# One fused attention and gated feed-forward kernel: a new planner order, pair sums, normalisation on three engines

## The chip, the cores and the metric
The kernel runs on one core of a Trainium2 chip. The metric is the device time of one execution in microseconds: 446.09 us, the median of three runs (445.58 to 446.64).

## What is computed
Attention over 4 batches, 8 heads, 768 positions and 64 columns, where a query sees the 96 positions up to its own and the first 8 keys, with a distance bias; its output feeds a feed-forward part (512 to 1024 to 512) with a gate.

```
scores = q @ k.T / 8 + bias            # bias = -2**-(h+1) * distance, -1e9 where not kept
a = exp(scores - max);  a = a / (sum(a) + 1e-9);  x = a @ v
h = relu(x @ w_in)                                   # 512 -> 1024
conv[s] = cw[0]*h[s-1] + cw[1]*h[s] + cw[2]*h[s+1]   # per column of h
out = (h * sigmoid(conv)) @ w_out                    # 1024 -> 512
```

w_in, conv_w and w_out arrive in double precision. Products are made in three parts of a high and a low half, so that they keep float32's precision.

## The kernel before, in words
The work is cut into 32 attention jobs (batch, half of the sequence, pair of heads) of three steps each, so 96 steps of 128 queries by two heads, and into 8 units of four jobs, each followed by its share of the feed-forward part. A step goes round the engines: TensorE makes both heads' scores (`s`, L512 to L515), VectorE adds the bias table and takes the maximum (L523), ScalarE takes the exponentials and their sums into columns of the small tile `mm` (L536), VectorE adds 1e-9 and inverts (`inverse`, L545 and L546), VectorE or GpSimd multiplies the weights by the inverse (`normalise`, L551), TensorE transposes them (`t`, L559 and L561), ScalarE evicts the transposes (`pt`, L566). Three steps make one product with v (`pv`, L576), whose high half ScalarE takes (`xh`, L586) and whose low half VectorE takes (`xl`, L591).

Of these, `mm1` (L602) makes the first feed-forward product in triples of matmuls per column block f of 8 and per job k of 4, into three accumulators; ScalarE's relu frees them (L610). Three taps follow per block: the middle one on GpSimd (L630), the outer two on VectorE (L632); then gate and saturation check on ScalarE, the gated product `c` (L664) and its low half `gl` (L682) on VectorE, and `mm2` (L692) makes the output tiles `o` of 24 matmuls. The very last tile is made in two halves `e` of 24 matmuls each (L720).

Sixteen pieces of the weights are taken apart during the first quarter (L445, L450, L455, L461). For a rare kind of input there is a general path behind a branch. Whether it is needed is found from the limits, the weights' words (16 checks, L477) and the saturation sums: VectorE reduces these (L481 to L490), one matmul sums the result over partitions (`total`, L771), VectorE writes the flag (L773), and all engines branch on it at the end.

The order on every engine is written by a planner (`Plan`, a list scheduler with hand-made costs and due times): each operation has an engine or a choice of engines, a cost, what it must follow, which buffers it takes, and when it is due; the cheapest start wins, and among those within 60 ns the earliest due. While the plan leaves TensorE a gap early on, filler matmuls on a zero tile (`warm`, L298) are put there. Loads go out on SyncE's queue, the first few also on ScalarE's.

Of the kernel before, what the change touches and what calls it, by code (L numbers as in the profile page):

```python
# [39 lines left out]
NPB, NPT = 4, 4  # L40
# [4 lines left out]
EARLY = 2  # L45
# [20 lines left out]
class Op:  # L66
    def __init__(self, key, eng, fn, after, alloc, use, due, behind):
        self.key, self.eng, self.fn, self.after, self.behind = key, eng, fn, after, behind
        self.alloc, self.use, self.due = alloc, use, due


RESULT = {"PE": 175, "ACT": 118, "DVE": 82, "POOL": 70, "SP": 900}
WAKE = {"PE": 45, "ACT": 45, "DVE": 45, "POOL": 90, "SP": 90}
ISSUE, SETUP, RATE = 570, 500, 270.0


class Plan:
# [8 lines left out]
    def best(self, free, taken):  # L86
        return self.arrange(free, taken)

    def arrange(self, free, taken):
# [21 lines left out]
        wire, port = free.pop("DMA"), {"DVE": 0.0, "POOL": 0.0}  # L111
        last_max, landed = False, [0.0] * LANES
        pe_gap = []
# [14 lines left out]
        while cand:  # L128
            best = None
            heads = {}  # L130
            for k in cand:
# [12 lines left out]
                for e, c in o.eng.items():  # L144
# [5 lines left out]
                    if c[1] and e in port:  # L150
                        t = max(t, port["POOL" if e == "DVE" else "DVE"])
# [5 lines left out]
            for e, hs in heads.items():  # L157
                t0 = min(h[0] for h in hs)
                _, due, k, c, t = min((h for h in hs if h[0] <= t0 + SLACK[e]), key=lambda h: (h[1], h[0]))
                if len(ops[k].eng) > 1:  # L160
                    mine = t + c[0]
                    others = [max(h[0], free[x]) + h[3][0] for x, g in heads.items() if x != e for h in g if h[2] == k]
# [11 lines left out]
            if k[0] in LOADS:  # L174
                free[e] = t + ISSUE
                wire = max(t + ISSUE + SETUP, wire) + c[0]
                end[k] = wire + RESULT["SP"]
                landed.append(end[k])
            else:
                free[e] = t + c[0]  # L180
                end[k] = t + c[0] + (150 if k[0] == "max" else RESULT[e])
                if c[1] and e in port:
                    port[e] = t + c[0]
# [22 lines left out]
EASY = 36000.0  # L206


def fast_path(tc, io):
# [43 lines left out]
    def load_q(m, j):  # L253
        b, u, hp = jobs[m]
        if m < NATIVE:
            r = slice(D * j, D * j + D)
            E = nc.sync if m else nc.scalar
# [31 lines left out]
    for m in range(2):  # L289
        zero_q(m)  # L290
# [3 lines left out]
    wp = ps_m.tile([P, 512], F32, tag="m", name="warm")  # L294

    def warm(n):
        for _ in range(n):
            T.matmul(wp[:, :P], wz, wz, start=True, stop=True)  # L298
# [20 lines left out]
    make_identity(nc, ident)  # L319
# [5 lines left out]
    V.tensor_scalar(lt, rel, 0.0, None, ALU.is_lt)  # L325
    nv = nn.rearrange("p (a b) -> p a b", a=2)
# [8 lines left out]
    W, M = slice(WIN, NT), slice(0, WIN)  # L335
    gW, gM = slice(WIN, WIN + NGLOB), slice(P - NGLOB, P)
# [7 lines left out]
    def nearer(r):  # L344
        V.tensor_scalar(rel[:, r], rel[:, r], nl, None, ALU.subtract)

# [4 lines left out]
    nearer(W)  # L351
    V.scalar_tensor_tensor(rel[:, gW], off[:, gW], 0.0, rel[:, gW], ALU.is_equal, ALU.mult)
    V.scalar_tensor_tensor(off[:, gW], keyf, ng, off[:, gW], ALU.is_ge, ALU.min)
    masked(W)
    for h in range(2):
        table(h, W)

    def middle():
        outside(M)
        nearer(M)  # L360
        V.memset(rel[:, gM], 0.0)
        V.tensor_scalar(off[:, gM], keyf, ng, None, ALU.is_ge)
        masked(M)
# [30 lines left out]

    cw = const.tile([P, 3 * NF], F32, name="cw")
# [18 lines left out]
    for t in pbuf:  # L414
        G.memset(t[:, 2 * WIN :], 0.0)

# [40 lines left out]
    def weight_low(i, half):  # L457
# [3 lines left out]
        V.tensor_tensor(l[:, sl], t, h[:, sl].bitcast(F32), ALU.subtract)  # L461
# [55 lines left out]
    def maximum(s, j):  # L517
        m, i, first, n = form(s)
        if j == 0:
            sums[s] = p1.tile([P, 8], F32, tag="mm", name=f"mm{s}", bufs=6)  # L520
# [12 lines left out]
    def exponentials(s, j):  # L533
# [4 lines left out]
            bias=mm[:, j : j + 1], scale=-1.0, accum_out=mm[:, 2 + j : 3 + j],  # L538
# [4 lines left out]
    def inverse(s):  # L543
        mm = sums[s]
        V.tensor_scalar(mm[:, 4:6], mm[:, 2:4], 1.0e-9, None, ALU.add)  # L545
        V.reciprocal(mm[:, 6:8], mm[:, 4:6])  # L546

    def normalise(s, j, eng):
        x = weights_of(s, j)
        X = V if eng == "DVE" else G  # L550
        X.tensor_scalar(x, x, sums[s][:, 6 + j : 7 + j], 1.0, ALU.mult, ALU.mult)  # L551

    def transposes(s, j):
        n = form(s)[3]
        pb = pbuf[s % NPB]
        if j == 0:
            st_pt[s] = ps_t.tile([P, 2, 2, P], F32, tag="t", name=f"t{s}")
        pt = st_pt[s]
        T.transpose(pt[:, 0, j], pb[:, j * WIN : j * WIN + P], ident)  # L559
        if n > P:  # L560
            T.transpose(pt[:, 1, j], pb[:, j * WIN + P : j * WIN + 256], ident)  # L561

    def evict(s):
        k = 1 if form(s)[2] else 2
        sb = p2.tile([P, 2, 2, P], F32, tag="pt", name=f"pt{s}", bufs=NPT)
# [3 lines left out]
    def values(m):  # L569
        pv[m] = ps_v.tile([P, TB], F32, tag="v", name=f"pv{m}")  # L570
        for i in (NB - 1, *range(NB - 1)):
            whole = form(NB * m + i)[2]
            sb = st_pt.pop(NB * m + i)
            for c, n, q in ((0, P, 0),) if whole else ((0, P, 0), (1, NLATE, NEAR)):
                for j in range(2):
# [3 lines left out]
                        sb[:n, c, j, q:],  # L579
# [16 lines left out]
    def mm1(n, f, k):  # L596
        if k == 0:
            hist["h", n, f] = ps_m.tile([P, 512], F32, tag="m", name=f"h{n}_{f}")
        ps = hist["h", n, f]
# [21 lines left out]
    def tap(n, f, k):  # L621
# [7 lines left out]
        if k == 1:  # L629
            G.tensor_scalar(c, h, x, 1.0, ALU.mult, ALU.mult)  # L630
# [44 lines left out]
    def low_g(n, t):  # L675
# [6 lines left out]
        V.tensor_tensor(  # L682
# [82 lines left out]
    def verdict():  # L765
        check_weights()
        check_gates()
        total = ps_v.tile([P, 512], F32, tag="v", name="total")
        E = mybir.EngineType
        hint = lambda e: tc.mark_branch_hint_location("general", "LikelyTaken", [e])  # L770
        T.matmul(total[0:1, 0:1], bad, ones, start=True, stop=True)  # L771
        hint(E.PE)
        V.tensor_scalar(flag[0:1], total[0:1, 0:1], 0.5, None, ALU.is_gt)  # L773
        hint(E.DVE)

    plan = Plan(dict(s=2, t=2, v=1, m=3, xh=6, xl=6, gh=4, gl=4, rk=1, rq=1, kk=2, ql=2, qh=2,
                     vv=2, pt=NPT, pb=NPB, mm=6, c=1, ob=1), ("ob",))
    add = plan.add
    act = lambda n, sb=0, bias=0, acc=0: ("ACT", (n * 0.833 + 50 + 45 * sb + 95 * bias + 93 * acc, 0))
    dve = lambda n: ("DVE", (n * 1.042 + 70, 1))  # L780
# [15 lines left out]
    for m in range(len(jobs)):  # L796
        native, w = m < NATIVE, NKC[jobs[m][1]]
        D0 = due_of(NB * m)
        if native:
# [4 lines left out]
            add(("ldk", m), ("SP", (P * w * 4 / RATE, 0)), (load_k, m), alloc=() if m % 2 else (bk,), use=(bk,), due=D0 - 9000)  # L804
            for j in range(2):
                add(("ldq", m, j), ("SP" if m else "ACT", (D * TB * 4 / RATE, 0)), (load_q, m, j),
# [336 lines left out]
```

## Time and profile before
| | |
|---|---|
| median of three runs | 446.09 us (445.58 to 446.64) |
| the profiled execution | 446.33 us |
| its span | 444.5 us |
| mean granted clock of TensorE | 0.992 of full |
| instructions | 8851 |
| HBM read, written | 52.95 MB, 6.29 MB |

The profile covers one execution. Busy time counts an engine's own instructions. Matmuls overlap, and their ends are modelled: what a matmul costs is the distance between two starts. "Idle before" names the engine whose result ended the wait.

### The profile page before, as it was taken

How to read it: one execution, taken by the hardware profiler on the slowest of the kernel's cores; microseconds unless marked ns; L12 is line 12 of the kernel's file. 1: busy time of each engine (PE TensorE's matmuls, PEld its weight loads, DVE VectorE, ACT ScalarE, POOL GpSimd, SP SyncE). 2: the span in 40 equal slices, each digit the busy share in tenths (PEclk: the TensorE clock that was granted, in tenths of full speed). 3: DMA queues.
4: the chain of work that ended last, by engine and by line, in shares of the span. 5: the costliest groups of instructions: out<-in, count | busy, mean ns of one | idle time of the engine just before them, and what ended most of it. 6: DMA issues, size and time to landing. Idle time of an engine off the chain costs nothing.

```text
span 444.5 us, 8851 instructions
## 1 busy us (share of the span) xinstructions
PE 427.6 (96%) x3034; PEld 379.6 (85%) x3034; DVE 375.0 (84%) x1047; ACT 281.0 (63%) x743; POOL 152.8 (34%) x243
## 2 busy tenths in 40 slices
PE   7999999999989999999999999999999999799896
PEld 6888988898889887999889888999889988698686
DVE  5799999999899979998998979898999798888700
ACT  1778877796488646875587547776478568545211
POOL 5545643414812372136402351227311540032000
PEclk8999999999999999999999999999999999999899
DMA  8887943233416133433443134433433042676011
GB/s 239 243 301 212 298 135 111 74 108 119 142 59 202 35 113 140 133 110 119 141 142 114 44 104 145 134 108 119 142 142 100 20 155 81 225 236 209 33 49 52
DMA packets 22515, 59.87 MB, mean 135 GB/s; under 512 B 2880, under 2 KB 5440, under 8 KB 22464
## 3 DMA queue, kind: packets, MB, share of 16 engines
q1 hardware_dynamic: 21872, 58.79, 41.0%
q8 instruction: 25, 0.41, 0.4%
q10 hardware_dynamic: 592, 0.46, 0.4%
q14 instruction: 26, 0.21, 0.1%
HBM read 52.95 MB, written 6.29 MB: 133 GB/s over the span
## 4 chain that ended last, share of the span: by engine, by line
PE 54%; DVE 32%; ACT 6%; DMA 4%; issue 3%; POOL 1%; ACTq 0%; DVEq 0%; SPq 0%
PE h L602 19%; PE o L692 17%; DVE c L632 6%; DVE s L523 5%; PE pv L576 4%; DVE pbuf L551 4%; ACT pbuf L536 3%; PE t L559 3%; PE s L514 2%; PE s L515 2%; DVE w L450 2%; PE t L561 2%; DVE mm L545 2%; DVE c L664 2%; DVE kk L274 2%
## 5 line engine op out<-in xcount | busy, mean ns | idle before, releaser
L536 ACT ACTIVATE pbuf<-s,mm 128x232 f32<-128x232 f32 (+1 forms) x192 | 82.8, 437 | 60.5 <-DVE mm L523 53.2
L602 PE MATMUL h<-xh,wih 128*128 128x384 f32 x256 | 92.0, 360 | 1.7 <-ACT xh L586 1.7
L602 PE MATMUL h<-xl,wih 128*128 128x384 f32 x256 | 86.6, 338 | 1.8 <-DVE xl L591 1.7
L602 PE MATMUL h<-xh,wil 128*128 128x384 f32 x256 | 86.2, 337 | 0.0
L523 DVE CUSTOM_DVE_ANT_0 s<-s,tab 128x232 f32<-128x232 f32 (+1 forms) x192 | 73.2, 382 | 13.0 <-PE s L515 7.4
L551 POOL TENSOR_SCALAR pbuf<-pbuf,mm 128x232 f32<-128x232 f32 (+1 forms) x67 | 38.5, 579 | 130.3 <-DVE mm L546 92.2
L632 DVE SCALAR_TENSOR_TENSOR c<-hbuf,cw,c 128x382 f32<-128x382 f32 (+1 forms) x128 | 76.1, 624 | 2.8 <-POOL c L630 2.6
L692 PE MATMUL o<-woh,gh 128*128 128x512 f32 x184 | 76.6, 416 | 0.0
L692 PE MATMUL o<-wol,gh 128*128 128x512 f32 x184 | 73.2, 398 | 0.0
L692 PE MATMUL o<-woh,gl 128*128 128x512 f32 x184 | 73.2, 398 | 0.0
L566 ACT ACTIVATE pt<-t 128x512 f32<-128x512 f32 (+1 forms) x96 | 53.2, 561 | 28.7 <-PE t L561 27.3
L630 POOL TENSOR_SCALAR c<-hbuf,cw 128x382 f32<-128x382 f32 (+1 forms) x64 | 44.5, 705 | 28.8 <-ACT hbuf L610 19.6
L602 PEld LDWEIGHTS h<-xh,wih 128*128 128x128 f32 x256 | 48.4, 189 | 3.3 <-ACT xh L586 2.1
L602 PEld LDWEIGHTS h<-xl,wih 128*128 128x128 f32 x256 | 48.3, 189 | 3.1 <-DVE xl L591 2.8
L559 PE MATMUL t<-ident,pbuf 128*128 128x128 f32 x192 | 47.8, 279 | 2.6 <-DVE pbuf L551 2.3
L551 DVE TENSOR_SCALAR pbuf<-pbuf,mm 128x232 f32<-128x232 f32 (+1 forms) x125 | 48.8, 418 | 0.8
L270 POOL CAST kk<-rk 128x1008 fp32r<-128x1008 f32 (+1 forms) x23 | 24.5, 1067 | 72.3 <-PE s L515 57.8
L602 PEld LDWEIGHTS h<-xh,wil 128*128 128x128 f32 x256 | 48.1, 188 | 0.0
L576 PEld LDWEIGHTS pv<-pt,v 128*64 128x64 f32 (+1 forms) x704 | 36.1, 136 | 8.9 <-issue 3.5
L576 PE MATMUL pv<-pt,v 128*64 128x128 f32 (+1 forms) x704 | 42.6, 267 | 1.0 <-ACT pt L566 1.0
L610 ACT ACTIVATE hbuf<-h 128x384 f32<-128x384 f32 x64 | 31.4, 492 | 17.7 <-PE h L602 17.7
L692 PEld LDWEIGHTS o<-woh,gl 128*128 128x128 f32 x184 | 34.9, 190 | 8.4
(99 smaller groups left out, 839.1 us busy)
## 6 DMA issues: line engine op xcount, KB each, us to landing
v<-in_vv SPq DMA_DIRECT2D x32, 384.0 KB, 3.9
rq<-in_qk SPq DMA_DIRECT2D x23, 384.0 KB, 4.0
check<-in_w SPq DMA_DIRECT2D x16, 512.0 KB, 4.4
wr<-in_w SPq DMA_DIRECT2D x16, 511.6 KB, 4.3
rk<-in_qk SPq DMA_DIRECT2D x12, 504.0 KB, 3.5
out<-ob SPq DMA_DIRECT2D x23, 256.0 KB, 2.2
rk<-in_qk SPq DMA_DIRECT2D x11, 400.0 KB, 3.2
rq<-in_qt SPq DMA_DIRECT2D x16, 96.0 KB, 5.4
```

The source lines that it names most:

```text
L270: G.tensor_copy(kk, raw[m, "k"])
L523: V.tensor_tensor_reduce(out=o, in0=o, in1=tab[:, h, WIN:] if first else tab[:, h, 0:WIN], scale=-0.125, scalar=3.0e38, op0=ALU.add, op1=A ...
L536: last_exp[s] = A.activation(weights_of(s, j), st_s[s][:, j, :n], AF.Exp, bias=mm[:, j : j + 1], scale=-1.0, accum_out=mm[:, 2 + j : 3 + j],)
L551: X.tensor_scalar(x, x, sums[s][:, 6 + j : 7 + j], 1.0, ALU.mult, ALU.mult)
L559: T.transpose(pt[:, 0, j], pb[:, j * WIN : j * WIN + P], ident)
L566: A.activation(sb[:, :k], st_pt[s][:, :k], AF.Copy)
L576: T.matmul(pv[m][64 * j : 64 * j + 64, i * P + q : (i + 1) * P], vt[m][:n, i, c, 64 * j : 64 * j + 64], sb[:n, c, j, q:], start=c == 0, st ...
L602: T.matmul(ps[:, :TB], w_[:, k, f * P : (f + 1) * P], x_, start=part == 0 and k == 0, stop=part == 2 and k == NK - 1,)
L610: A.activation(hbuf[:, f, c : c + TB], hist["h", n, f][:, :TB], AF.Relu, scale=0.5)
L630: G.tensor_scalar(c, h, x, 1.0, ALU.mult, ALU.mult)
L632: V.scalar_tensor_tensor(c, h, x, c, ALU.mult, ALU.add)
L692: T.matmul(ps, g_[:, f], w_[:, f], start=f == 0 and part == 0, stop=f == NF - 1 and part == 2,)
```

## The change
What it does, part by part; order counts are for the path that is taken.

- *Pair sums.* Six fixed `mm` tiles get 1e-9 beside each of the two sums once; `inverse` then adds each pair by a TENSOR_REDUCE instead of adding 1e-9 by a TENSOR_SCALAR.
- *Normalising also by ScalarE.* `normalise` may go to ScalarE, and the middle tap too. By the order, the 192 normalisations lie 91 on VectorE, 33 on GpSimd and 68 on ScalarE (before 125, 67, 0), the 64 middle taps 37 on GpSimd and 27 on ScalarE (before 64, 0). Ahead of the maximum of step 42 VectorE has 34 normalisations and 45 outer taps (before 55 and 32).
- *Verdict in three pieces*: VectorE's reductions, the matmul, the flag, each with its own place.
- *Two slices side by side.* In each unit the first two blocks of `mm1` (three in the first unit, before two) go job by job instead of one after the other.
- *First loads in fixed order*; the second half of the first q moves from ScalarE's queue to SyncE's; the zeros of the first q tiles come after the position numbers on GpSimd; a dummy exponential loads ScalarE's table.
- *Shorter table.* Two wide passes over the distances become two of 8 columns; the second head's first table is made after the first maximum. The filler writes into the first accumulator of `h`; 158 fillers follow the first 40 (before 184).
- *The planner* counts what VectorE and GpSimd lose beside each other, costs DMAs by rows and size, sets due times backwards from the end of its own plan, and repeats that up to six times.

```
-RESULT = {"PE": 175, "ACT": 118, "DVE": 82, "POOL": 70, "SP": 900}
+RESULT = {"PE": 175, "ACT": 118, "DVE": 82, "POOL": 70, "SP": 700}
...
     def best(self, free, taken):
-        return self.arrange(free, taken)
+        found = self.arrange(free, taken)
+        for _ in range(ROUNDS):
+            self.latest(*found)
+            again = self.arrange(free, taken)
+            if again[1] < found[1]:
+                found = again
+            else:
+                break
+        return found
...
+            if e == "DVE" and c[1] and port["POOL"] > t:
+                return port["POOL"] - t if c[1] == 1 else 70.0
+            if e == "POOL" and c[1]:
+                x = port["slow"]
+                return min(max(0.0, port["DVE"] - t) * x, c[0] * x / (1 - x))
...
-            E = nc.sync if m else nc.scalar
+            E = nc.sync if m + j else nc.scalar
...
+    mmb = [const.tile([P, 8], F32, name=f"mm{i}") for i in range(NMM)]
+    for t in mmb:
+        G.memset(t[:, 2:6], 1.0e-9)
...
-            bias=mm[:, j : j + 1], scale=-1.0, accum_out=mm[:, 2 + j : 3 + j],
+            bias=mm[:, j : j + 1], scale=-1.0, accum_out=mm[:, 2 + 2 * j : 3 + 2 * j],
...
-        V.tensor_scalar(mm[:, 4:6], mm[:, 2:4], 1.0e-9, None, ALU.add)
-        V.reciprocal(mm[:, 6:8], mm[:, 4:6])
+        pairs = mm[:, 2:6].rearrange("p (j t) -> p j t", t=2)
+        V.tensor_reduce(mm[:, 0:2], pairs, axis=mybir.AxisListType.X, op=ALU.add)
+        V.reciprocal(mm[:, 6:8], mm[:, 0:2])
...
+        if eng == "ACT":
+            A.activation(x, x, AF.Copy, scale=y)
...
+            if eng == "ACT":
+                A.activation(c, h, AF.Copy, scale=x)
...
-    def verdict():
-        check_weights()
-        check_gates()
...
+        if k == 0:
+            check_weights()
+            check_gates()
+        elif k == 1:
+            hist["total"] = ps_v.tile([P, 512], F32, tag="v", name="total")
+            T.matmul(hist["total"][0:1, 0:1], bad, ones, start=True, stop=True)
...
+    first = [("ldk", 0), ("ldq", 0, 1), ("ldk", 1), ("ldq", 1, 0), ("ldq", 1, 1), ("ldv", 0), ("wl", order[0])]
...
-        e = EARLY if n == 0 else 0
+        e = EARLY if n == 0 else LATE
...
-    add(("ver",), ("DVE", (1500, 0)), (verdict,), [("chk", NCHK - 1), ("xl", len(jobs) - 1)] + [("sat", n, k) for n in range(NU) for k in range(NG)],
-        (("v", "total"),), (("v", "total"),), at - 8000)
+    add(("ver", 0), ("DVE", (1500, 0)), (verdict, 0), [("chk", NCHK - 1)] + [("sat", n, k) for n in range(NU) for k in range(NG)], due=at - 8000)
+    add(("ver", 1), ("PE", (130, 0)), (verdict, 1), [("ver", 0), ("xl", len(jobs) - 1)], (("v", "total"),), (("v", "total"),), at - 4500)
+    add(("ver", 2), ("DVE", (200, 0)), (verdict, 2), [("ver", 1)], (), (("v", "total"),), at - 4000)
```

Three places show how rows move. ScalarE around the exponentials of steps 13 and 14, first before, then now (`pbuf` are the weights, `hbuf` the relu's output, L621 the normalisation).

```order
L536 ACTIVATE pbuf1_177,mm13_752<-s13_741,mm13_752 128x232 x2
...
L566 ACTIVATE pt13_867<-t13_856 128x512
L445 ACTIVATE w4_0_878<-wr4_0_695,misc_163 128x512
L536 ACTIVATE pbuf3_179,mm15_865<-s15_829,mm15_865 128x232 x2
L610 ACTIVATE hbuf_173<-h0_0_484 128x384
L610 ACTIVATE hbuf_173<-h0_1_513 128x384
```

```order
L604 ACTIVATE pbuf1_176,mm1_184<-s13_754,mm1_184 128x232 x2
L449 ACTIVATE setup_84<-setup_84,misc_152 128x24
L659 ACTIVATE xh3_831<-pv3_800 128x384
L621 ACTIVATE pbuf1_176<-pbuf1_176,mm1_184 128x232
L604 ACTIVATE pbuf2_177,mm2_185<-s14_790,mm2_185 128x232 x2
L639 ACTIVATE pt12_859<-t12_824 128x512
L639 ACTIVATE pt13_865<-t13_846 128x512
L685 ACTIVATE hbuf_172<-h0_0_532 128x384
L621 ACTIVATE pbuf2_177<-pbuf2_177,mm2_185 128x232
L685 ACTIVATE hbuf_172<-h0_1_542 128x384
```

Two normalisations now stand in ScalarE's line, ahead of evictions and relus, and each needs VectorE's inverse of its step. TensorE around the last job's product `pv31`, first before, then now (`t95` the last transposes, `xh31` and `xl31` the two halves of that product).

```order
L602 MATMUL h7_0_4955<-xh30_4840,wil_170 128x384
L559 MATMUL t95_4979<-ident_142,pbuf3_179 128x128
L561 MATMUL t95_4979<-ident_142,pbuf3_179 128x128
L559 MATMUL t95_4979<-ident_142,pbuf3_179 128x128
L561 MATMUL t95_4979<-ident_142,pbuf3_179 128x128
L576 MATMUL pv31_4990<-pt95_4987,v31_4757 64x128 x2
...
L576 MATMUL pv31_4990<-pt94_4933,v31_4757 64x104 x2
L602 MATMUL h7_0_4955<-xh31_5008,wih_169 128x384
```

```order
L634 MATMUL t95_4856<-ident_136,pbuf3_178 128x128
L677 MATMUL h7_0_4866<-xh28_4444,wih_168 128x384
...
L677 MATMUL h7_0_4866<-xh29_4636,wil_169 128x384
L649 MATMUL pv31_4885<-pt95_4870,v31_4634 64x128 x2
...
L649 MATMUL pv31_4885<-pt94_4821,v31_4634 64x104 x2
L677 MATMUL h7_1_4875<-xh29_4636,wih_168 128x384
...
L677 MATMUL h7_1_4875<-xh30_4765,wil_169 128x384
L677 MATMUL h7_0_4866<-xh31_4902,wih_168 128x384
```

Three triples that don't need the last job now stand between its transposes and its product, and three more between the product and the first triple that needs it. TensorE around the verdict's matmul `total`, first before, then now.

```order
L692 MATMUL o3_2_5246<-woh_171,gl3_2_5003 128x512
L771 MATMUL total_5260<-misc_163 1x1
L692 MATMUL o3_2_5246<-woh_171,gh3_2_4975 128x512
```

```order
L770 MATMUL o3_4_5205<-woh_170,gl3_4_5132 128x512
L851 MATMUL total_5233<-misc_152 1x1
L798 MATMUL e3_5_0_5238<-woh_170,gh3_5_5154 128x256
```

It moved past 69 matmuls of three output tiles, to just ahead of the two halves of the last tile.

## Rows read from the trace of the kernel before
**Rows 1.** The page: engines' busy time, and the chain that ended last, by engine.
```profile
PE 427.6 (96%) x3034; PEld 379.6 (85%) x3034; DVE 375.0 (84%) x1047; ACT 281.0 (63%) x743; POOL 152.8 (34%) x243
...
PE 54%; DVE 32%; ACT 6%; DMA 4%; issue 3%; POOL 1%; ACTq 0%; DVEq 0%; SPq 0%
```
**Rows 2.** Busy time by stage: length, then PE, PEld, DVE, ACT, POOL; clock, DMA.
```profile
0.00:20.00 20.00, 16.88 (x175) 15.57 (x177) 12.77 (x58) 7.85 (x27) 10.50 (x42) 0.91 0.81 245
20.00:140.00 120.00, 116.26 (x934) 104.84 (x929) 115.16 (x353) 89.64 (x254) 54.59 (x77) 1.00 0.49 159
140.00:380.00 240.00, 238.23 (x1633) 210.40 (x1632) 213.45 (x583) 161.82 (x430) 80.00 (x116) 1.00 0.36 115
380.00:420.00 40.00, 35.55 (x191) 31.29 (x190) 32.76 (x56) 19.14 (x33) 7.75 (x9) 0.96 0.56 179
```
**Rows 3.** Busy time of the filler matmuls alone by stage: length, then PE.
```profile
0.00:20.00 20.00, 10.22 (x126) 0.91 0.81 245
20.00:60.00 40.00, 7.12 (x98) 1.00 0.80 255
```
**Rows 4.** Groups by line, VectorE: shapes and count; busy us, mean ns; idle before.
```profile
L632 DVE SCALAR_TENSOR_TENSOR c<-hbuf,cw,c 128x382 f32<-128x382 f32 (+1 forms) x128 | 76.1, 624 | 2.8 <-POOL c L630 2.6
...
L551 DVE TENSOR_SCALAR pbuf<-pbuf,mm 128x232 f32<-128x232 f32 (+1 forms) x125 | 48.8, 418 | 0.8
...
L545 DVE TENSOR_SCALAR mm<-mm 128x2 f32<-128x2 f32 x96 | 24.8, 258 | 15.6 <-ACT pbuf L536 15.0
```
**Rows 5.** Timeline, VectorE, first 24 us: start, duration, instruction, idle before.
```profile
3.44 0.40 DVE L320 CAST setup<-reli 128x360 f32<-128x360 int32 x1 [3.44 <-POOL reli L315]
...
7.95 0.30 DVE L523 CUSTOM_DVE_ANT_0 s<-s,tab 128x128 f32<-128x128 f32 x1 [0.89 <-PE s L512]
...
13.11 0.16 DVE L545 TENSOR_SCALAR mm<-mm 128x2 f32<-128x2 f32 x1
...
20.13 0.52 DVE L545 TENSOR_SCALAR mm<-mm 128x2 f32<-128x2 f32 x1
...
23.76 0.16 DVE L380 TENSOR_REDUCE misc<-misc 128x1 f32<-128x3 f32 x1
```
**Rows 6.** Timeline, GpSimd, the same stretch.
```profile
0.87 0.41 POOL L236 MEMSET rq<- 64x384 f32 x1
...
20.01 0.61 POOL L455 CAST wih<-w 128x512 fp32r<-128x512 f32 x1
...
23.50 0.46 POOL L551 TENSOR_SCALAR pbuf<-pbuf,mm 128x232 f32<-128x232 f32 x1 [0.39 <-DVE mm L546]
```
**Rows 7.** Groups by line, ScalarE: an exponential and a gate.
```profile
L536 ACT ACTIVATE pbuf<-s,mm 128x232 f32<-128x232 f32 (+1 forms) x192 | 82.8, 437 | 60.5 <-DVE mm L523 53.2 <-POOL pbuf L551 2.5 <-POOL kk L270 1.9
...
L640 ACT ACTIVATE c<-c 128x764 f32<-128x764 f32 (+1 forms) x32 | 27.1, 849 | 7.6 <-DVE c L632 7.5
```
**Rows 8.** Timeline, TensorE, last job and verdict.
```profile
384.43 1.42 PE L576 MATMUL pv<-pt,v 128*64 128x128 f32 x24 [0.83 <-ACT pt L566]
386.44 0.45 PE L602 MATMUL h<-xh,wih 128*128 128x384 f32 x1 [0.59 <-ACT xh L586]
387.83 0.44 PE L602 MATMUL h<-xl,wih 128*128 128x384 f32 x1 [0.94 <-DVE xl L591]
...
416.98 0.19 PE L771 MATMUL total<-misc 128*1 128x1 f32 x2 [2.09 <-DVE misc L490]
...
417.70 0.63 PE L692 MATMUL o<-wol,gh 128*128 128x512 f32 x1
418.12 0.63 PE L692 MATMUL o<-woh,gl 128*128 128x512 f32 x1
```
**Rows 9.** The chain that ended last, in time: start, length, matmuls back to back.
```profile
131.18 3.18 PE h L602 x18
...
170.67 3.50 PE o L692 x15
```
**Rows 10.** Busy time by stage behind the verdict, as rows 2.
```profile
418.00:420.00 2.00, 2.00 (x6) 1.52 (x6) 0.88 (x2) 1.06 (x1) 0.00 (x0) 0.50 0.01 4
```

## What was predicted, with its working
> **What bounds the kernel now.** I read the page's engine table first, then the busy time by stage, then the groups by line, and last the timeline at the places where TensorE stands still. The table says that TensorE is busy 427.6 of 444.5 us, and the chain that ended last runs over it for 54% and over VectorE for 32% [rows 1]. TensorE's 96% flatters it: 17.34 us of its busy time are filler matmuls on a zero tile [rows 3]. So 444.5 - 427.6 + 17.3 = 34.2 us hold no real work, and the stages say where [rows 2, 3]. In 0:20 it is 20 - 16.88 + 10.22 = 13.3 us. In 20:140 it is 3.7 of idle and 7.1 of filler, 10.9. In 140:380 it is only 1.8. In 380:420 it is 4.5, and the last 24.5 us hold the remaining 3.9, nearly all of it the last store. The reader is to see that VectorE is the pacemaker exactly where TensorE lacks work: 115.16 of 120 us in 20:140, against 213.45 of 240 later. ScalarE has 89.64 of 120 there. So the change can win on the ramp until about 140 us, at the two stalls near the end, and hardly anything between. The 410 us of real matmuls are the same in both kernels, and the order on TensorE keeps nearly the same mix: the scores of step 42 have the same work ahead of them in both.
>
> **The sums of pairs.** Before, 1e-9 is added by a TENSOR_SCALAR on two columns: 96 of them, 258 ns in the mean [rows 4]. One that meets no GpSimd work takes 0.16 us (at 13.11). The one at 20.13 takes 0.52 us, and ends when GpSimd's cast, which began at 20.01 and takes 0.61, ends [rows 5, 6]. So 96 x (258 - 160) = 9.4 us of VectorE's time is waiting for GpSimd. The new form is a TENSOR_REDUCE. The trace has one beside GpSimd: at 23.76, inside GpSimd's TENSOR_SCALAR of 23.50 to 23.96, it takes 0.16 us as if alone [rows 5, 6]. I therefore take the whole 9.4 as gone; on one example, zero is the other bound. The Trainium skill, page "SBUF — State Buffer", section "Who interferes with whom", states that on this chip a tensor_reduce never contends with GpSimd, while a tensor_scalar can; by it the 9.4 us go in full, and the one row agrees.
>
> **The normalisations.** 192 remain. By the order, VectorE keeps 91 of 125, GpSimd 33 of 67, and ScalarE takes 68. The middle taps were all GpSimd's 64; now ScalarE does 27. VectorE loses 34 x 418 ns = 14.2 us over the run [rows 4]. ScalarE has no such row. Its nearest are the exponential of the same shape at 437 ns and a 128x764 pass from SBUF to SBUF at 849 [rows 7]; I take 0.44 us for a normalisation, and 0.53 for a tap of 382 columns, a little above the first. The Trainium skill, page "ScalarE: Activation LUTs", section "What ACT_TABLE_LOAD costs", speaks against this price: 186 ns plus 0.833 ns a column, plus 93 for a scale read from a column, an estimate of 472 ns at 232 columns. By it ScalarE's 68 cost some 2 us more in all.
>
> **The ramp.** What counts is VectorE's queue ahead of a step that TensorE waits for. I take the maximum of step 42, close behind the end of the 20:140 stage. By the order, 55 normalisations stood ahead of it and now 34 do: 21 x 418 = 8.8 us less. 42 pair sums give 42 x 98 = 4.1. Against that, 45 outer taps stand ahead of it where 32 did, 13 x 624 = 8.1 more [rows 4]. Net 4.8 us. Those taps feed the second product, and may lie in VectorE's gaps: then the ramp wins 12.9. Or ScalarE's new work takes the place of what went: then it wins 0. I take **-4.8 us**, because charging the taps in full is the careful side of rows that are all measured.
>
> **The start.** GpSimd writes four zero halves from 0.87 on, 0.41 us each, ahead of the position numbers, so VectorE's first cast waits for those until 3.44 [rows 5, 6]. Now the numbers come first, some 4 x 0.41 = 1.6 us sooner, and one 8-column pass and one table stand where a 128-column pass and two tables stood. The first maximum was held by its scores all the same, 0.89 us until 7.95 [rows 5]: the second half of q was the second load in ScalarE's queue, behind which SyncE had already started the v tile and the convolution weights. Now it is SyncE's second load, and those follow later. Both paths shorten, the limit values are still needed in between, so I take **-1.2 us** (0 to -2).
>
> **The middle**, 140:380, holds 1.8 us, many short waits. Fewer waits for normalised tiles, more queue on ScalarE: **-1.0** (0 to -1.8).
>
> **The last attention job.** TensorE stands 0.83 us for an eviction, 0.59 for the high half and 0.94 for the low half of its result [rows 8], 2.4 in all. Now the last transposes stand three triples earlier, and three triples that need neither half stand behind the product, where none stood. A triple takes 0.53 us (18 matmuls in 3.18 us [rows 9]), so 1.6 us cover each gap. The eviction is hidden. The two halves are covered but for some 0.5 us, since VectorE has four weight checks in its queue first. **-1.6** (0 to -2.4).
>
> **The verdict.** The matmul that sums the faults stood in the output tiles with 69 + 48 matmuls behind it, and waited 2.09 us for VectorE's reductions [rows 8]. Behind it the granted clock was 0.50 in 418:420, that is the lower of the two levels [rows 10]: an output matmul started every 0.42 us (417.70 to 418.12 [rows 8]) instead of every 0.233 (15 in 3.50 us [rows 9]). Until about 420.3 that makes eight intervals, 8 x 0.19 = 1.5 us lost. Now the sum stands after all 128x512 output tiles, 69 x 0.233 = 16.1 us of matmuls later, and its inputs are long there. Nothing is late in its place: behind the sum the old trace has no further wait of TensorE. **-3.7** (at least -2.1, if the clock falls anyway). The flag has the last 48 matmuls beside it. The check loads, the shorter table and the dummy exponential lie beside DMA and engines that wait there: nothing.
>
> **Sum**: -1.2 - 4.8 - 1.0 - 1.6 - 3.7 = -12.3; 444.5 - 12.3 = 432.2 of span. The profiled execution took 446.33 with that span, 1.8 outside it: 434.0. It lies 0.24 above the median of 446.09, so **433.8 us**. With every term at its near end (0 and -2.1) it is 444; at its far end, -22.8, it is 423.3.
>
> **Rivals.**
> 1. *The ramp stays.* ScalarE takes 32 normalisations and 10 taps ahead of step 42. That is 32 x 0.44 + 10 x 0.53 = 19.4 us on top of 89.64 in 20:140, 109 of 120: two in-order engines that wait for each other at about 90%. Start, last job and verdict remain: 444.5 - 6.5 = 438.0, or 439.6. The same comes out if the pair sums still wait for GpSimd. For it: the order pulls taps forward. Against: VectorE's waits on GpSimd are measured, and GpSimd has 61 fewer instructions. 438 to 443.5: 0.22.
> 2. *The ramp opens fully.* The taps fall into gaps: 12.9 instead of 4.8 gives 425.7; 423 to 429: 0.12.
> 3. *Slower: ScalarE's queue blocks.* A normalisation on ScalarE waits in line for the reciprocal, and evictions and relus wait behind it, which free TensorE's accumulators; the order shows this at steps 13 and 14. If each of the 32 holds the queue for a pair sum and a reciprocal, 0.33 us, ScalarE comes to 109 + 10.6 = 119.6 of 120: the point from which it decides. At twice that wait 10.6 us go straight to TensorE, and the 6.5 of start, last job and verdict stay: 444.5 + 10.6 - 6.5 = 448.6, or 450.2. For it: 25 fewer of 184 fillers show no such gap, so it would be a surprise to the order too. 0.08.
> 4. *The clock.* After a pause of 2.09 us TensorE ran at the lower level [rows 8, 10]. The new order has fewer fillers in the ramp, 158 after the first 40 where there were 184, and none from step 15 on. The Trainium skill, page "TensorE: Matmul & The Clock Gate", section "HAM oscillation — how this bites in real kernels", says that each long pause makes the clock fall and the work behind it start slow again. Three such pauses would cost 3 x 1.5 = 4.5 us: 438.3. Against it: in 20:140 the clock was 1.00 throughout [rows 2]. 0.04.
> 5. *Nothing to measure*, because gains and new waits cancel: 0.04.
>
> **How the numbers follow.** My forecast, 429 to 438, has what is left, 0.50. Faster by over 0.2% (about what a measurement of this kernel can tell from no change, here 0.9 us) are the forecast and rivals 1, 2 and 4: 0.88. Within it 0.04, slower 0.08. The range of 426 to 443 leaves out half of rival 2, the slower rival and the edge of rival 1.
>
> **What would show it.** Right: the pair sums at about 0.16 to 0.19 us whatever GpSimd does, a verdict matmul without a wait and a clock of 1.00 behind it, some 1 us of waits around the last job, a first maximum near 6.7, and filler plus idle in 20:140 near 6. Wrong: ScalarE above 110 us in 20:140 with TensorE waiting for evictions or relus, or VectorE still above 95% there.

## The result, and the profile after

| | before | changed |
|---|---|---|
| median of 4 runs | 445.86 us | 439.76 us (439.52 to 440.48) |
| ratio, 95% interval | | 0.986, 0.985 to 0.988 |
| profiled execution, span | 446.33, 444.5 us | 439.52, 437.7 us |

The change is 6.1 us faster, half of the 12.3 that the sum gave. The experiments ran on several chips, on which the kernel before took 445.4 to 447.1 us; so each is told by its ratio to it, and in us of 445.9.

The page of the changed kernel, its engine table and the chain by engine, the lines that answer to [rows 1]:

```profile
PE 424.0 (97%) x3008; PEld 375.1 (86%) x3008; DVE 364.4 (83%) x1013; ACT 319.1 (73%) x839; POOL 129.1 (29%) x187
...
DVE 40%; PE 38%; ACT 9%; issue 4%; DMA 4%; POOL 3%; SPq 0%; POOLq 0%; DVEq 0%; ACTq 0%
```

Its stages (columns as in [rows 2]), then the filler matmuls alone (length, PE, PEld). They are taken by their source line, L363, because 23 of the 198 write into the first accumulator of `h` and don't bear the name `warm` of [rows 3]:

```profile
0.00:20.00 20.00, 18.45 (x224) 17.30 (x224) 15.63 (x64) 11.81 (x37) 11.36 (x48) 1.00 0.90 281
20.00:140.00 120.00, 116.35 (x886) 104.93 (x885) 115.52 (x351) 107.11 (x296) 48.34 (x62) 1.00 0.50 159
140.00:380.00 240.00, 235.57 (x1608) 206.44 (x1607) 204.66 (x552) 178.00 (x470) 66.63 (x74) 1.00 0.37 112
380.00:420.00 40.00, 39.79 (x214) 34.70 (x213) 28.45 (x48) 20.22 (x35) 2.78 (x3) 1.00 0.56 185
...
0.00:20.00 20.00, 11.69 (x160) 10.98 (x160) 1.00 0.90 281
20.00:60.00 40.00, 2.99 (x40) 2.46 (x39) 1.00 0.71 233
```

Idle plus filler of TensorE, against [rows 2, 3]: in 0:20 13.3 and now 20 - 18.45 + 11.69 = 13.2; in 20:140 10.9 and now 120 - 116.35 + 2.99 = 6.6; in 140:380 1.8 and now **4.4**; in 380:420 4.5 and now 0.2. The gains came where they were looked for, the ramp's smaller than forecast. The middle, where nothing was to be had, lost 2.7 us. These differences make 5.9 us less, and with the 1.5 of lower clock behind the old verdict 7.4; the span fell by 6.8. The rest lies in short delays between matmuls that busy time covers: counted from start to start, against the usual pace of each kind of matmul, the middle lost some 4 us (an estimate), 1.3 more than its idle time shows.

Who made TensorE wait stands in its groups by line. The transposes in 20:380, before and then after:

```profile
L559 PE MATMUL t<-ident,pbuf 128*128 128x128 f32 x183 | 45.6, 279 | 2.6 <-DVE pbuf L551 2.3
...
L561 PE MATMUL t<-ident,pbuf 128*128 128x128 f32 x154 | 38.8, 278 | 0.7 <-DVE pbuf L551 0.7
```

```profile
L632 PE MATMUL t<-ident,pbuf 128*128 128x128 f32 x180 | 45.6, 280 | 4.6 <-DVE pbuf L624 4.4
...
L634 PE MATMUL t<-ident,pbuf 128*128 128x128 f32 x153 | 38.9, 277 | 1.1 <-POOL pbuf L624 1.0
```

The waits for normalised tiles grew from 3.3 to 5.7 us. One of them on the timeline of the changed kernel, rows of VectorE, GpSimd and TensorE:

```profile
227.64 0.17 DVE L615 RECIPROCAL mm<-mm 128x2 f32<-128x2 f32 x1
...
227.82 1.02 POOL L337 CAST kk<-rk 128x1008 fp32r<-128x1008 f32 x1 [1.92 <-PE s L583]
227.84 1.14 DVE L624 TENSOR_SCALAR pbuf<-pbuf,mm 128x232 f32<-128x232 f32 x1
...
229.12 0.30 PE L632 MATMUL t<-ident,pbuf 128*128 128x128 f32 x1 [0.95 <-DVE pbuf L624]
```

GpSimd's cast begins 0.02 us ahead of VectorE's normalisation, which then takes 1.14 us; the 48 that meet no GpSimd work take 0.33 in the mean. The transposes behind it stand for 0.95 us. VectorE's and ScalarE's groups, to set against [rows 4, 7]:

```profile
L710 DVE SCALAR_TENSOR_TENSOR c<-hbuf,cw,c 128x382 f32<-128x382 f32 (+1 forms) x128 | 83.0, 673 | 3.9 <-POOL c L708 3.1
...
L624 DVE TENSOR_SCALAR pbuf<-pbuf,mm 128x232 f32<-128x232 f32 (+1 forms) x91 | 34.5, 394 | 1.0
...
L614 DVE TENSOR_REDUCE mm<-mm 128x2 f32<-128x4 f32 x96 | 14.5, 151 | 10.5 <-ACT pbuf L604 9.8
```

```profile
L621 ACT ACTIVATE pbuf<-pbuf,mm 128x232 f32<-128x232 f32 (+1 forms) x68 | 31.9, 484 | 18.1 <-DVE mm L615 17.7
...
L706 ACT ACTIVATE c<-hbuf,cw 128x382 f32<-128x382 f32 (+1 forms) x27 | 16.5, 618 | 0.7 <-DVE gl L760 0.2
```

The pair sums cost 10.3 us less and the normalisations 14.3 less, as forecast. But VectorE's busy time fell by 10.6, not 24.6: the outer taps, the same 128 instructions, went from 76.1 to 83.0 us, the gate's subtractions and products and the k subtractions grew by 6 more. Before, 17 outer taps lay beside GpSimd work; now it is 40, at 804 ns in the mean where the other 88 take 613.

### The profile page after: what moved, and what is told of

The parts are those of the page before. It is cut to its first block, busy times and chain, and to the rows that moved or that the text cites. A ratio compares the mean times of both kernels' runs of the same rounds, so it can differ in the third digit from the quotient of the medians.

```text
span 437.7 us, 8864 instructions
## 1 busy us (share of the span) xinstructions
PE 424.0 (97%) x3008; PEld 375.1 (86%) x3008; DVE 364.4 (83%) x1013; ACT 319.1 (73%) x839; POOL 129.1 (29%) x187
## 4 chain that ended last, share of the span: by engine, by line
DVE 40%; PE 38%; ACT 9%; issue 4%; DMA 4%; POOL 3%; SPq 0%; POOLq 0%; DVEq 0%; ACTq 0%
PE o L770 15%; DVE c L710 10%; PE h L677 8%; DVE s L591 6%; DVE c L742 4%; DVE kk L341 4%; DMA check<-in_w 4%; PE pv L649 3%; DVE gl L760 3%; ACT pbuf L604 2%; PE s L580 2%; DVE pbuf L624 2%; ACT sat L725 2%; DVE ql L349 2%; PE t L632 2%
## 5 line engine op out<-in xcount | busy, mean ns | idle before, releaser
L710 DVE SCALAR_TENSOR_TENSOR c<-hbuf,cw,c 128x382 f32<-128x382 f32 (+1 forms) x128 | 83.0, 673 | 3.9 <-POOL c L708 3.1
L770 PE MATMUL o<-woh,gh 128*128 128x512 f32 x184 | 76.1, 413 | 0.0
L639 ACT ACTIVATE pt<-t 128x512 f32<-128x512 f32 (+1 forms) x96 | 53.8, 564 | 10.3 <-PE t L634 9.3
L708 POOL TENSOR_SCALAR c<-hbuf,cw 128x386 f32<-128x386 f32 (+1 forms) x37 | 31.2, 847 | 88.1 <-ACT hbuf L685 78.6
L624 POOL TENSOR_SCALAR pbuf<-pbuf,mm 128x232 f32<-128x232 f32 (+1 forms) x33 | 23.3, 705 | 103.9 <-DVE mm L615 80.1
L632 PE MATMUL t<-ident,pbuf 128*128 128x128 f32 x192 | 48.4, 280 | 4.6 <-DVE pbuf L624 4.4
L337 POOL CAST kk<-rk 128x1008 fp32r<-128x1008 f32 (+1 forms) x23 | 26.9, 1168 | 65.3 <-PE s L583 54.9
L621 ACT ACTIVATE pbuf<-pbuf,mm 128x232 f32<-128x232 f32 (+1 forms) x68 | 31.9, 484 | 18.1 <-DVE mm L615 17.7
L634 PE MATMUL t<-ident,pbuf 128*128 128x128 f32 x160 | 40.6, 276 | 1.1 <-POOL pbuf L624 1.0
```

The costliest lines, as they stand in the source:

```text
L621: A.activation(x, x, AF.Copy, scale=y)
L624: X.tensor_scalar(x, x, y, 1.0, ALU.mult, ALU.mult)
L632: T.transpose(pt[:, j * P : (j + 1) * P], pb[:, j * WIN : j * WIN + P], ident)
L634: T.transpose(pt[:, (2 + j) * P : (3 + j) * P], pb[:, j * WIN + P : j * WIN + 256], ident)
L639: A.activation(sb[:, :k], st_pt[s][:, :k], AF.Copy)
L710: V.scalar_tensor_tensor(c, h, x, c, ALU.mult, ALU.add)
```

## The experiments

The theories. **B2**: the planner now lays VectorE and GpSimd side by side at a price that is too low, tiles come later than its plan says, and TensorE waits for them. Rivals: ScalarE's new work (R), due times that leave no slack, and pair sums whose wait only moved on (B).

**e1_pairs_alone.** The kernel before with the new pair sums only:

```
-        V.tensor_scalar(mm[:, 4:6], mm[:, 2:4], 1.0e-9, None, ALU.add)
+        V.tensor_reduce(mm[:, 0:2], pairs, axis=mybir.AxisListType.X, op=ALU.add)
```

> The kernel before with the pair sums as TENSOR_REDUCE on six fixed tiles that hold 1e-9 beside each sum, in the order of before. Theory A (the wait for GpSimd is gone for good): 96 pair sums fall from 24.8 us of VectorE to about 14.5, VectorE's busy time from 375 to about 365, and what of it lies ahead of step 42 (42 x 0.1 = 4.1 us) comes off the ramp: 441.5 to 444. Theory B (the wait moves on to the instruction of VectorE behind it, an outer tap, a normalisation or a subtraction): the pair sums at 14.5, but the outer taps above their 624 ns and the other groups longer by some 5 to 9 us together, the time within 1 us of 445.9.

Ratio 0.989 (0.986 to 0.992), -4.8 us. VectorE's two lines:

```profile
L637 DVE SCALAR_TENSOR_TENSOR c<-hbuf,cw,c 128x382 f32<-128x382 f32 (+1 forms) x128 | 76.8, 629 | 2.7 <-POOL c L635 2.5
...
L550 DVE TENSOR_REDUCE mm<-mm 128x2 f32<-128x4 f32 x96 | 14.5, 151 | 16.5 <-ACT pbuf L540 16.0
```

Theory A holds and B falls: the wait is gone for good, and the taps stay at 629 ns. But idle plus filler in 20:140 fell only from 10.9 to 10.1. The order is that of before, so the two profiled executions can be set side by side matmul by matmul: TensorE is 1.0 us ahead at 133 us, 2.8 at the verdict's matmul, and 4.4 at the end. The last 1.5 us are not the pair sums. The verdict's matmul waits as long as before, but the granted clock stays at 1.00 behind it, where [rows 10] has 0.50 (a row of TensorE's timeline, then its stages: length, PE, clock, DMA):

```profile
414.14 0.19 PE L776 MATMUL total<-misc 128*1 128x1 f32 x2 [2.12 <-DVE misc L494]
...
416.00:418.00 2.00, 2.00 (x10) 1.00 0.01 4
418.00:420.00 2.00, 2.00 (x11) 1.00 0.01 4
```

So the pair sums by themselves are worth some 3 us here, and a pause of 2.1 us does not lower the clock every time.

**e2_pairs_undone.** The changed kernel in its own order, with the old pair sums:

```
-        V.tensor_reduce(mm[:, 0:2], pairs, axis=mybir.AxisListType.X, op=ALU.add)
+        V.tensor_scalar(mm[:, 0:2], pairs[:, :, 0], 1.0e-9, None, ALU.add)
```

> The changed kernel, its order kept, with the pair sums as TENSOR_SCALAR that adds 1e-9 again. Theory A: 96 x 0.1 us come back, half of them on the ramp, which grows by 3 to 5 us: 442.5 to 445. Theory B: the pair sums take 20 to 26 us again, the outer taps fall from 673 ns towards 624 and GpSimd's casts too, and the time stays within 1.5 us of 439.8.

Ratio 0.989 (0.986 to 0.992), 1.1 us above the changed kernel; the two intervals overlap. The profiled spans differ by 3.2 (440.9 and 437.7). The pair sums took 19.6 us, 5.1 more; the taps stayed at 670 ns, so this is not B's moving wait either, and A's ramp of 3 to 5 us more did not come in full. In the new order the new form is worth 1 to 3 us, which is no clear difference from the 3 in the old one.

**e3_verdict_alone.** The kernel before with `verdict(k)` in three pieces and its three `add` lines, as in the diff.

> The kernel before with the verdict in three pieces as in the changed kernel, nothing else; its sum then stands behind the 128x512 output tiles. Forecast's term: the 2.09 us of wait and 1.5 us of the lower clock go, 3.6 off: 442.3, granted clock 1.00 in 418:420. Rival: the clock falls there anyway or the wait turns up elsewhere near the end: 443.5 to 445.9.

Ratio 0.991 (0.988 to 0.994), -3.9 us. By stage (columns as in [rows 2]):

```profile
418.00:420.00 2.00, 2.00 (x11) 1.59 (x10) 1.23 (x1) 0.64 (x2) 0.00 (x0) 1.00 0.07 29
```

The verdict's term was right in size and cause: matmul by matmul, in the order of before, TensorE gains 2.4 us at the place of the wait and 1.6 behind it. Another 1.2 us of the profiled difference lie in the first 21 us, where this execution has a clock of 1.00 and that of before 0.91 [rows 2].

**e4_apart.** The changed kernel, its planner with the old rule for the two engines:

```
-            if e == "DVE" and c[1] and port["POOL"] > t:
-                return port["POOL"] - t if c[1] == 1 else 70.0
...
+                    if c[1] and e in port:
+                        t = max(t, port["POOL" if e == "DVE" else "DVE"])
```

> The changed kernel, whose planner again never lays an instruction of VectorE that reads two SBUF operands or is a scalar one beside one of GpSimd (the rule of before), everything else as changed. Theory B2 (the new planner lays the two engines side by side, and both are slower for it: outer taps 673 instead of 624 ns, GpSimd's q casts 1134 instead of 946, and this gave back 4 us between 140 and 380): the groups fall to their times of before, TensorE's waits for normalisations in 140:380 shrink, 436 to 439. Rival (the waits in the middle come from due times that leave the transposes no slack, or from ScalarE): per instruction times fall, the time stays at 439 to 442, because the plan now makes the engines take turns.

Ratio 0.961 (0.958 to 0.964): **-17.3 us**, 11.2 under the changed kernel, more than B2 gave. Middle (columns as in [rows 2]) and transposes:

```profile
140.00:380.00 240.00, 239.11 (x1662) 212.40 (x1661) 206.04 (x548) 194.36 (x509) 54.06 (x68) 1.00 0.38 124
```

```profile
L620 PE MATMUL t<-ident,pbuf 128*128 128x128 f32 x184 | 45.7, 279 | 0.1
...
L622 PE MATMUL t<-ident,pbuf 128*128 128x128 f32 x156 | 39.1, 275 | 0.2
```

The waits for normalised tiles fell from 5.7 us to 0.3, the middle's idle time from 4.4 to 0.9. But VectorE's groups did not all fall to their times of before, as B2 had it: the outer taps did nearly, at 633 ns, while the k subtractions rose (1154 ns before, 1247 in the changed kernel):

```profile
L329 DVE TENSOR_TENSOR kk<-rk,kk 64x1008 fp32r<-64x1008 f32 (+1 forms) x23 | 33.2, 1443 | 1.6 <-POOL kk L325 1.1
```

This plan also gives ScalarE more (90 normalisations and 35 middle taps, where it had 68 and 27): rival R, for the next ones.

**e5_side_no_scalar** takes `"ACT"` out of both choices of the changed kernel; **e6_apart_no_scalar** does the same to e4_apart.

```
-                add(("nrm", s, j), {"POOL": (n * 0.86 + 233, 1, NRM_POOL), "DVE": (n * 0.521 + 130, 1), "ACT": (n * 0.833 + 145, 0, NRM_ACT)}, (normalise, s, j),
+                add(("nrm", s, j), {"POOL": (n * 0.86 + 233, 1, NRM_POOL), "DVE": (n * 0.521 + 130, 1)}, (normalise, s, j),
```

> The changed kernel with ScalarE left out of the normalisations and middle taps: 133 and 59 normalisations on VectorE and GpSimd, all 64 middle taps on GpSimd, the planner's new rule kept. If ScalarE's share is a gain (theory S, in which the two engines side by side are what costs): more of VectorE and GpSimd beside each other, the ramp and the middle grow, 444 to 450, ratio to before 0.995 to 1.01. If ScalarE's queue is what holds TensorE up in the middle (rival 3 of the forecast): 434 to 438, ratio 0.973 to 0.983.

> The planner's rule of before (e4_apart) and no normalisation or middle tap on ScalarE. Theory S (the rule costs some 10 us by itself): 7 to 14 us under e5_side_no_scalar. Theory R (taking turns only pays because ScalarE took 90 normalisations and 35 taps in e4_apart where the changed kernel gave it 68 and 27): within 3 us of e5_side_no_scalar.

e5: ratio 0.988 (0.984 to 0.992), 0.8 us above the changed kernel, and the intervals overlap; both guesses missed. e6: 0.975 (0.972 to 0.977), 6.0 us under e5, between the two guesses. But e6 does not compute the function (its relative error is 1.009; what goes wrong in it is not known), so its time is an indication at most: the rule would cost 6 us without ScalarE's help and 11.2 with it. (Each kernel is planned anew, so these are differences of whole plans.) e5's idle plus filler in 20:140 is 3.9 + 3.6 = 7.5 us, against the changed kernel's 6.6 and 10.9 before: the ramp's gain was for the most part not ScalarE's. e5 also has a new wait at the last job, TensorE's timeline:

```profile
386.77 0.44 PE L677 MATMUL h<-xl,wih 128*128 128x384 f32 x1 [2.22 <-DVE xl L664]
```

**e7_side_more_scalar.** The new rule kept, ScalarE's share raised to that of e4_apart:

```
-    NRM_POOL, NRM_ACT, TAP_ACT = 300.0, 200.0, 0.0
+    NRM_POOL, NRM_ACT, TAP_ACT = 600.0, 0.0, -300.0
```

> The changed kernel with its new rule, but ScalarE's penalties moved so that it gets 89 normalisations and 37 middle taps, nearly the share that it had in e4_apart (90 and 35). Theory S: within 3 us of the changed kernel, 437 to 442, ratio 0.980 to 0.991. Theory R: as e4_apart, 429 to 432, ratio 0.961 to 0.968.

Ratio 0.984 (0.981 to 0.986), as theory S had it. R falls: with the same share e4_apart stands 10 us lower. The transposes wait 7.1 us here (more than in the changed kernel, though the time is 1.2 us less), 5.1 of it in the first of their two lines, for all three engines that normalise:

```profile
L632 PE MATMUL t<-ident,pbuf 128*128 128x128 f32 x182 | 46.2, 281 | 5.1 <-ACT pbuf L621 3.3 <-POOL pbuf L624 1.1 <-DVE pbuf L624 0.6
```

**e8_side_margin.** `MARGIN["PE"]` of the changed kernel from 600 to 1500.

> The changed kernel with 1.5 us instead of 0.6 of slack that the planner wants for TensorE between an input and the matmul that reads it. If the waits between 140 and 380 are a lack of slack in the plan (the instructions take longer than planned, TensorE has other work that could stand ahead): 436 to 438, the middle's waits for normalisations down by half. If slack is not to be had there: 439 to 442.

Ratio 0.992 (0.989 to 0.995), 2.5 us slower than the changed kernel. The middle did as the slack theory said, and the ramp paid for it:

```profile
20.00:140.00 120.00, 113.83 (x862) 102.47 (x862) 115.99 (x349) 103.67 (x289) 45.62 (x62) 0.99 0.51 158
140.00:380.00 240.00, 238.28 (x1643) 210.42 (x1639) 201.60 (x548) 184.79 (x485) 73.20 (x71) 1.00 0.36 112
```

Idle time in the middle is back at 1.7 us, and the transposes' waits fell from 5.7 to 3.2. But TensorE stands idle for 6.2 us in 20:140, where it was 3.7, and 1.58 more at the last job, so neither guess has the time. Slack only moves the cost.

**e9_price_250.** One number of the changed kernel:

```
-                return port["POOL"] - t if c[1] == 1 else 70.0
+                return port["POOL"] - t if c[1] == 1 else 250.0
```

> The changed kernel with one number: where VectorE's instruction of two SBUF operands would start beside one of GpSimd, the planner charges it 250 ns instead of 70 (the trace of the changed kernel has outer taps at 613 ns alone and 804 beside, the first product of the gate at 973 and 1377). Theory P (the rule is sound, its price too low): most of the way to e4_apart, 430 to 434, ratio 0.963 to 0.975. Theory Q (a price of its own is not enough, since the plan still lays them side by side wherever it sees a gap, and GpSimd's instructions lose too): 436 to 441, ratio 0.978 to 0.990.

Ratio 0.970 (0.964 to 0.975), -13.5 us: theory P. This number alone brings two thirds of the way to e4_apart. The transposes wait 2.3 us:

```profile
L632 PE MATMUL t<-ident,pbuf 128*128 128x128 f32 x184 | 46.2, 280 | 1.8 <-ACT pbuf L621 1.0 <-DVE pbuf L624 0.8
...
L634 PE MATMUL t<-ident,pbuf 128*128 128x128 f32 x156 | 39.3, 276 | 0.5 <-DVE pbuf L624 0.2
```

**e10_apart_late0.** `LATE` of e4_apart from 2 to 0.

> e4_apart with the first two blocks of each later unit's first product one after the other again, as before (three in the first unit as in the changed kernel). If the last job's three waits were worth the forecast's 1.6 us: ratio 0.0025 to 0.006 above e4_apart, that is 1 to 2.7 us, with waits of 0.5 to 0.9 us at the last product and its two halves. Rival: the waits are taken up by the end of the kernel, or the order has other cover: within 0.7 us of e4_apart.

Ratio 0.975 (0.969 to 0.980), 6.0 us above e4_apart; the profiled spans differ by 4.2. Both guesses missed: the last job shows no wait with either value,

```profile
380.00:420.00 40.00, 40.00 (x194) 34.83 (x193) 24.69 (x42) 19.94 (x34) 1.00 (x1) 1.00 0.43 150
```

and most of what can be placed lies in the ramp: idle plus filler in 20:140 grows from 3.8 to 6.4 us, idle in 140:380 from 0.9 to 1.2. Two blocks side by side pay, but not by covering the last job's waits; by what, stays open.

**e11_apart_due_by_hand.** `ROUNDS` of e4_apart from 6 to 0.

> e4_apart with the due times by hand and one pass of the planner, as before, instead of due times set backwards and repeated. If the backward due times are worth something the forecast did not price: 432 to 437, the ramp longer. If not: within 1 us of e4_apart. If they hurt: 427 to 429.

Ratio 0.958 (0.953 to 0.963), **427.0 us**, with e12 the fastest of all, with 240.00 of 240 us busy in the middle. That lies where due times that hurt would put it, but the interval overlaps e4_apart's (0.958 to 0.964): the backward due times bring nothing that these runs show.

**e12_apart_less_scalar.** e4_apart with `NRM_ACT, TAP_ACT = 700.0, 3000.0`.

> e4_apart with ScalarE's penalties raised so that it gets 62 normalisations and 17 middle taps, fewer than in the changed kernel (68 and 27). Theory S (taking turns is what counts): 430.5 to 434, ratio 0.964 to 0.975. Theory R (e4_apart won by ScalarE's larger share): 437 to 440, ratio 0.981 to 0.988.

Ratio 0.959 (0.953 to 0.964), 427.4 us, lower than either guess, with less work on ScalarE than in the changed kernel. R falls a second time. Its outer taps warn against the simple reading of B2:

```profile
L698 DVE SCALAR_TENSOR_TENSOR c<-hbuf,cw,c 128x382 f32<-128x382 f32 (+1 forms) x128 | 80.7, 662 | 1.8 <-ACT c L694 1.3 <-POOL c L696 0.4
```

```profile
L620 PE MATMUL t<-ident,pbuf 128*128 128x128 f32 x184 | 44.7, 278 | 0.7 <-ACT pbuf L609 0.7
```

The taps are nearly as long as in the changed kernel (44 lie beside GpSimd work), and yet the transposes wait 0.7 us. VectorE time lost beside GpSimd is not what the end is paid in; what counts is whether the tiles that TensorE waits for come when the plan says. That can be looked up.

**Plan against trace.** The plan that each run's kernel.py makes names a time for every operation, and the order on every engine, so that the plan's operations and the trace's can be paired one by one. Worked out from the two, for the normalised tiles in 140:380: by how much a tile came later than planned, counted against TensorE's own place in the plan (good to about 0.1 us), and how many came too late for the slack that the plan had left. Last, the plan's own end and the profiled span.

| | later than planned: median, nine tenths under | too late | plan's end | span | over the plan |
|---|---|---|---|---|---|
| before | 0.32, 0.91 us | 6 of 112 | 421.4 us | 444.5 us | 23.1 us |
| changed | 0.61, 1.12 | 13 of 110 | 420.9 | 437.7 | 16.8 |
| e5, no ScalarE | 0.32, 1.11 | 8 of 112 | 421.5 | 440.7 | 19.2 |
| e7, more ScalarE | 0.43, 1.01 | 6 of 110 | 418.1 | 436.9 | 18.8 |
| e8, more slack | 0.42, 1.21 | 3 of 112 | 424.5 | 442.1 | 17.6 |
| e9, price 250 | 0.15, 0.57 | 5 of 112 | 420.1 | 429.5 | 9.4 |
| e6, turns, no ScalarE (output wrong) | 0.32, 0.96 | 6 of 112 | 419.7 | 434.7 | 15.0 |
| e4, turns | 0.02, 0.27 | 3 of 112 | 417.9 | 427.4 | 9.5 |
| e10, turns | 0.05, 0.69 | 2 of 112 | 422.4 | 431.6 | 9.2 |
| e11, turns | 0.01, 0.33 | none of 112 | 418.8 | 426.2 | 7.4 |
| e12, turns | -0.04, 0.42 | 1 of 110 | 418.3 | 426.3 | 8.0 |

The plans' own ends lie within 7 us of each other. What parts the orders at the price of 70 (changed, e5, e7, e8) from those with turns or the price of 250 that use ScalarE (e4, e9 to e12) is how far the chip falls behind them, 17 to 19 us against 7 to 9.5. Turns alone don't do it: the kernel before and e6 take turns without ScalarE's help, and fall behind by 23.1 and 15.0. A new plan can move the time by several us for other reasons (e10 stands 6.0 us above e4), but the two groups don't overlap: ratios 0.984 to 0.992 against 0.958 to 0.975.

## Why the prediction was right, and where it was not

**The direction and the range held, the likeliest case didn't**: 439.8 lies in the range (426 to 443) but outside the forecast's own 429 to 438, at the place of rival 1 (438 to 443.5), though not by its mechanism: the ramp did not stay. That the range held says little for the working, since it is wide enough to hold a loss that no term foresaw: of the missing 6.2 us some 1.7 lie in start and ramp and some 5 in the middle (4 lost instead of 1.0 won), and the last job gave 0.8 back.

- *The verdict, -3.7.* Right: e3 measures -3.9 (-2.5 to -5.2). In the changed kernel the sum stands at 427.84 without a wait, at a clock of 1.00. That the clock falls behind such a wait is not certain, as e1 shows; the 1.5 us are what it cost in the profiled execution.
- *The ramp, -4.8, and the start, -1.2.* Too large together: idle plus filler until 140 us fell by 4.3, forecast 6.0, and the forecast's own mark, the maximum of step 42, starts at 148.74 instead of 151.45, 2.7 earlier. The first maximum starts at 6.01, earlier than the 6.7 expected; how much of that is the clock, 1.00 in 0:20 where it was 0.91, is not known (e3 gained 1.2 us there with the order of before). The working was wrong too: it credited normalisations moved to ScalarE and pair sums. e5 has most of the ramp's gain without ScalarE's share, and in e1 the pair sums give 0.8 us there. What carries the rest (the third accumulator that the filler no longer holds, three blocks side by side, the order of loads) was not tried apart. Two small misreadings change nothing: 26 fillers fewer, not 25, and the pair sum at 13.11 begins beside the end of a GpSimd memset (12.78, 0.41 us).
- *The last job, -1.6.* The three waits of [rows 8], 2.4 us, are gone, the far end of the term. Not shown as to cause: e10 lacks the two blocks side by side and has no wait there, while e5 and e8 have them and wait 2.22 and 1.58 us for the low half. It depends on what the plan leaves in VectorE's queue.
- *The pair sums' 9.4 us.* Right as VectorE's time: 10.3 us less. The Trainium skill, page "SBUF — State Buffer", section "Who interferes with whom", says that a tensor_reduce never contends here; the traces agree: the 22 of the 96 that overlap GpSimd work take 147 ns in the mean, the other 74 take 152. As TensorE's time they are worth some 3 us in the old order (e1's 4.8 less the 1.5 of the clock behind the verdict) and 1 to 3 in the new.
- *ScalarE's prices.* A normalisation takes 484 ns, not 440, and a tap 618, not 530. The Trainium skill's page "ScalarE: Activation LUTs", section "What ACT_TABLE_LOAD costs", gave an estimate of 472 for the first; the trace is nearer to it than to the row that I took. ScalarE came to 107.1 us in 20:140, forecast 109, below the point of rival 3. The sign "VectorE above 95%" was a bad one: it is at 96% and the ramp is shorter all the same.
- **The step that failed is "The middle ... -1.0"**, with the premise of "VectorE loses 14.2 us": that every instruction left on VectorE and GpSimd keeps its duration and comes when it is needed. The planner's new rule stands in the description of the change, and the forecast has no term for it. It lets an instruction of two operands start beside GpSimd's for 70 ns, where the outer taps of this trace lose 191. The middle's idle time grew by 2.7 us instead of falling by 1.0. e4, e9 and e12 show the cause from three sides: turns, a higher price, turns with less of ScalarE. Without the new rule the change is worth 17.3 us.

That TensorE waits because tiles come later than planned is shown for the changed kernel's middle: the 13 tiles that came too late did so by 3.7 us in all, and TensorE stood for 3.2 us before transposes there. The waits alone don't rank the kernels: e7 has longer ones than the changed kernel and is faster, and in e8 other waits took their place. Which instruction's overrun made most of the tiles late stays open.

## What to carry to other kernels

A planner's cost numbers are part of the change: price each by a row of the trace and ask what the new order will lay side by side that the old one kept apart. Time lost on an engine with slack says little; look for the consumer that waits, here the transposes, and count its waits before and after. Where the order is a plan, set the plan's times beside the trace's. Gains of parts do not simply add up: e1's gain and e3's both hold the 1.5 us of lower clock behind the verdict, in the profiled executions. And count by source line, not by a tile's name, when the change renames what a group writes to, as it did here with the filler.

## What the runs showed of the hardware

GpSimd can hold VectorE for much longer than an instruction: a 128x232 normalisation took 1.14 us beside a cast of 1.02, where the 48 of the changed kernel that meet no GpSimd work take 0.33. The loss goes the other way too: GpSimd's middle taps went from 705 ns to 847 in the mean in the changed kernel, and there the 24 of 37 that overlap a TENSOR_TENSOR or SCALAR_TENSOR_TENSOR of VectorE take 966, the other 13 take 628.

```profile
L708 POOL TENSOR_SCALAR c<-hbuf,cw 128x386 f32<-128x386 f32 (+1 forms) x37 | 31.2, 847 | 88.1 <-ACT hbuf L685 78.6 <-DVE mm L614 4.4 <-DVE gl L760 2.7
```
